# A new order list for a retention and SwiGLU kernel: same operations, other sequence, other engines, other PSUM banks

## The chip, the cores and the metric

The kernel runs on one core of a Trainium2 chip. That core has a matrix engine (TensorE, PE in the profile), three engines that work on tiles (VectorE, or DVE; ScalarE, or ACT; GpSimd, or POOL), a queue engine that only starts transfers (SyncE, or SP), and 16 DMA engines that carry them out. The metric is the device time of one execution in microseconds (us). Less is better.

## The reference

q, k and v have the shape (4 batches, 8 heads, 768 positions, 64 channels). A retention layer runs over the positions, and a SwiGLU block with an RMS norm runs over its output, which is seen as 3072 rows of 512 channels (8 heads x 64):

```python
for t in range(S):                                     # gamma_h = 1 - 2**(-5-h)
    state = gamma * state + einsum('bhd,bhe->bhde', k[:, :, t], v[:, :, t])
    y[:, :, t] = scale * einsum('bhd,bhde->bhe', q[:, :, t], state)
x = y.transpose(0, 2, 1, 3).reshape(3072, 512)
xn = x / sqrt(mean(x * x, -1) + 1e-6) * rms_g
g = xn @ w_gate                                        # 512 x 1536
out = (g * sigmoid(g) * (xn @ w_val)) @ w_out          # 1536 x 512
```

## The kernel before, in words

The positions are cut into six groups c = 0 to 5 of 128 positions. A group has one block of 128 rows per batch b, so one group is 512 rows. Inside a block the recurrence is written as a masked product of scores, and a state per batch carries the past from group to group. The feed-forward block then runs over the 512 rows of the group: twelve slices of 128 hidden channels, each with four matmuls of 128x512 for the gate and four for the value, and then twelve matmuls of 128x512 per batch for the output.

The whole program is one string, ORDER (line 17). It has 867 words, one operation each, and a loop at the end of the function emits them in turn. A word reads `name.c.b/banks@engine>gate`. The numbers behind the name are the group, the batch and further arguments. The digits behind "/" are the PSUM banks that the operation writes. "@D", "@A", "@P" and "@S" stand for DVE, ACT, POOL and SP. ">name" lets a transfer wait for another operation. No planner stands behind it: each engine carries out its own words strictly in the order of the string, and an engine that waits for one word holds back all of its later words. An operation that writes a bank waits for the last reader of that bank, and a tile of a ring in SBUF is reused after its last reader.

The words that this text uses, with the line of the instruction that the profile shows:

- L (Lq, Lk, Lv) loads a block of q, k or v (L312, L314). On SP it arrives in f32 in a ring (four buffers each for q and k, six for v); on POOL the transfer casts to bf16 on its way. wg, wv and wo load slices of the weights, on POOL (L325, L332).
- Cq, Ck and V cast the f32 blocks to bf16, q and v with their decay (L341, L145, L360; V on ACT is eight small activations, L358).
- Tq and Tk transpose on PE (L368 for blocks loaded in another layout, L373), and Eq and Ek evacuate the result. tq and tk are DMA transposes on SP (L389), for the groups from c = 2 on.
- mk0 and mk1 compute the first group's decay masks on ACT (L268) from a row mask that the word iota makes on POOL; mc multiplies the second group's mask (L281); causal makes the 0/1 mask on POOL (L253).
- A computes scores (L405, two banks per batch), M0 and M1 multiply them by the mask on DVE (L427), Y and Z compute the block's output (L442, L446).
- S, R and N are the norm: the squares' sum on ACT (L459), the root on POOL (L469, L471), and the scaled rows on DVE (L483). X and XE transpose those rows into xnT, on PE with an evacuation (L496, L145) in the groups 0 and 1 and as a DMA transpose on SP (L502) from c = 2 on.
- J and D prepare decayed k rows (L518); K, U and B bring the state up to date: matmuls (L529), an f32 sum or copy (L538, L145), a bf16 copy on POOL (L545).
- g and v are the gate and value matmuls (L553), s the Silu on ACT (L563), h the product on DVE (L571), d and e the output matmuls (L578; e, L600, in three cuts for the last block), o the evacuation of the output (L145, on DVE or ACT), st its store (L591). H and tab warm up PE and ACT's table.

`g.0.3.4.0.3/0` is thus the gate product of group 0, hidden slice 3 alone, batches 0 to 2, into bank 0. Group 0's feed-forward work is cut into such pieces, so that it can start before all of its batches are there.

Of the kernel before, what the change touches and what calls it, by code (L numbers as in the profile page):

```python
# [17 lines left out]
Lk.0.2@S H.4/4 yd causal Lv.0.2@S>causal yt rms.1@S ident Ck.0.2@A Lq.0.0@P H.8/1 Lq.0.1@P Lq.0.2@P Tk.0.2/7  # L18
H.2/5 Lk.0.0@P Tq.0.1/0 vd Tq.0.0/4 Ek.0.2@D Lk.0.1@P Tq.0.2/1 Lk.0.3@P G/7 V.0.2@D Eq.0.1@D Tk.0.0/0 Tk.0.1/6
Eq.0.2@D Eq.0.0@D iota Lq.0.3@P A.0.2/31 Lv.0.1@P mk0 Lv.0.0@P Lv.0.3@P Ek.0.0@D mk1 GE@A wg.0.2 M1.0.2 wv.0.2  # L20
H.2/4 M0.0.2 Ek.0.1@A A.0.0/5270 D.0.2@P M1.0.1 Tk.0.3/6 Y.0.2/1 Tq.0.3/0 M0.0.1 H.2/4 tab Lk.1.1@P M1.0.0
M0.0.0 S.0.2 Ek.0.3@A J.0.0/4 J.0.1/7 R.0.2 Y.0.1/2 Eq.0.3@A S.0.1 H.1/6 H.3/0 H.1/5 D.0.0@D Y.0.0/3 N.0.2
J.0.3/5 D.0.1@D wv.2.4 R.0.1 X.0.2/6 N.0.1 S.0.0 wg.2.4 A.0.3/41 R.0.0 X.0.1/0 XE.0.2@A wg.4.6 D.0.3@D M0.0.3
XE.0.1@A g.0.0.2.2.3/2 K.0.2.2/5 K.0.0.2/6 M1.0.3 U.0.2.2@A s.0.0.2.2.3 N.0.0 v.0.0.2.2.3/7 g.0.0.2.1.2/0
h.0.0.2.2.3 Y.0.3/5 Lq.1.0@P wv.4.6 X.0.0/3 U.0.0.2@A S.0.3 wg.6.9 Tk.1.1/4 v.0.0.2.1.2/2 XE.0.0@D s.0.0.2.1.2
h.0.0.2.1.2 g.0.0.2.0.1/6 R.0.3 wv.6.9 Ek.1.1@A v.0.3.4.0.3/3 v.0.2.3.0.3/4 N.0.3 g.0.3.4.0.3/0 Lk.1.2@P
s.0.0.2.0.1 X.0.3/6 v.0.0.2.0.1/5 XE.0.3@A Lk.1.0@P B.0.0 wg.9.12 s.0.3.4.0.3 Lq.1.1@P g.0.5.6.0.3/1
g.0.2.3.0.3/7 h.0.3.4.0.3 s.0.2.3.0.3 Lq.1.2@P h.0.2.3.0.3 g.0.4.5.0.3/0 wv.9.12 h.0.0.2.0.1 s.0.4.5.0.3
v.0.0.4.3.4/2 g.0.0.4.3.4/7 v.0.4.5.0.3/3 mc.1@P s.0.5.6.0.3 s.0.0.4.3.4 h.0.0.4.3.4 wo.0.4 v.0.5.6.0.3/4
# [36 lines left out]
d.2.3.0.12/1 d.2.2.0.12/2 U.3.0.2@D g.3.0.1.0.4/4 v.3.0.1.0.4/7 Lq.4.0@S U.3.2.2@D st.0.2@S g.3.3.4.0.4/0
Ck.4.2@P s.3.3.4.0.4 st.0.1@S Lk.4.3@S Lv.5.0@S g.3.5.6.0.4/3 st.1.1@S B.3.1 v.3.3.4.0.4/0 d.2.1.10.12 tk.4.2
g.3.4.5.0.4/5 Cq.4.3@P Cq.4.1@D s.3.0.1.0.4 Lq.5.3@S o.2.3@A h.3.0.1.0.4 h.3.3.4.0.4 s.3.5.6.0.4 o.2.1@D
g.3.1.2.0.4/3 v.3.1.2.0.4/1 s.3.1.2.0.4 Ck.5.0@D o.2.2@D B.3.2 tq.4.2 V.4.3@P g.3.6.7.0.4/4 Lq.5.2@S V.4.2@P
Cq.4.0@P v.3.6.7.0.4/3 s.3.6.7.0.4 tq.4.0 h.3.1.2.0.4 v.3.5.6.0.4/0 g.3.2.3.0.4/2 h.3.5.6.0.4 Lk.5.1@S  # L70
h.3.6.7.0.4 tk.4.0 s.3.4.5.0.4 V.5.2@P tq.4.1 s.3.2.3.0.4 v.3.2.3.0.4/4 g.3.9.10.0.4/1 Ck.4.3@D v.3.4.5.0.4/0
Ck.5.1@D B.3.0 s.3.9.10.0.4 Lk.5.2@S g.3.10.11.0.4/1 Lk.5.3@S st.2.3@S h.3.4.5.0.4 Cq.5.3@P Lv.4.1@S A.4.0/0352
s.3.10.11.0.4 v.3.10.11.0.4/6 B.3.3 h.3.2.3.0.4 M0.4.0 M1.4.0 M0.4.1 M1.4.1 g.3.8.9.0.4/1 tq.4.3 v.3.9.10.0.4/7
Y.4.0/4 st.1.2@S tk.4.3 s.3.8.9.0.4 S.4.0 v.3.8.9.0.4/5 Cq.5.2@D st.2.1@S h.3.10.11.0.4 h.3.9.10.0.4
d.2.0.0.10/1 Lq.5.1@S R.4.0 N.4.0 Ck.5.2@A V.4.1@A A.4.2/6732 h.3.8.9.0.4 Lq.5.0@S M0.4.2 M1.4.2 Y.4.1/4
g.3.7.8.0.4/5 d.2.0.10.12 g.3.11.12.0.4/6 Cq.5.1@P Ck.5.3@D M1.4.3 K.4.2.2/7 o.2.0@A s.3.7.8.0.4 tq.5.2 M0.4.3
s.3.11.12.0.4 K.4.0.2/1 U.4.2.2@D Z.4.2/50 tq.5.3 v.3.7.8.0.4/2 tk.5.2 Y.4.3.2 Y.4.2.2 S.4.1 h.3.7.8.0.4
# [562 lines left out]
```

## Time and profile before

| | us |
|---|---|
| median of 3 runs | 232.16 (231.90, 232.18 and 232.16) |
| span of the profiled execution | 230.7 |
| what lies around that span, against the median | 1.46 |
| PE busy | 223.7 (97%) |
| DVE, ACT, POOL busy | 128.7, 87.8, 92.8 |
| granted PE clock | 1.00 throughout |

The profile gives the profiled execution's span, from its first to its last instruction; the times of the runs hold what lies around it too, so the two are compared through the difference in the table. The page gives busy times of each engine, the chain of work that ended last (followed back from the last instruction), groups of equal instructions with their mean duration and the idle time ahead of them, and DMA issues with the median time to landing. In a row of the timeline, the first number is the start, the second the duration, and the brackets hold the engine's idle time before it and what ended that. In a row of a table of stretches, the columns are the stretch, its length, and the busy time of PE, PE's weight loads, DVE, ACT and POOL with their numbers of instructions, then the PE clock, the DMA share and GB/s.

### The profile page before, as it was taken

The page shows a single profiled execution, that of the slowest core. Times are in us where ns is not written, and L with a number is a line of the kernel's source. Part 1 is how long each engine was busy: PE and PEld are TensorE (multiplying, and loading weights), DVE is VectorE, ACT ScalarE, POOL GpSimd, SP SyncE. Part 2 cuts the span into 40 slices and gives each one's busy share as a digit, 9 for nine tenths or more (in the row PEclk, how much of TensorE's full clock was granted, in tenths as well). Part 3 has the DMA queues.
Part 4 walks back from the last instruction along what each step waited for, and adds up shares of the span by engine and source line. Part 5 has one row for each costly group of instructions (what it writes and reads, how often), then busy time and mean ns, then how long its engine had stood idle before and what let it go on. Part 6 is the DMA issues. An engine that isn't in the chain of part 4 may idle for free.

```text
span 230.7 us, 4733 instructions
## 1 busy us (share of the span) xinstructions
PE 223.7 (97%) x1822; PEld 119.3 (52%) x1849; DVE 128.7 (56%) x239; ACT 87.8 (38%) x197; POOL 92.8 (40%) x163
## 2 busy tenths in 40 slices
PE   8989999999999999999999999999999999999994
PEld 2567755556564554445544445544554444444552
DVE  5797296937574876476670648856664325432200
ACT  6776524216424450344420435661354124222021
POOL 8979999124866235424349401339040000000000
PEclk9999999999999999999999999999999999999999
DMA  7999999999978946999999989774216200001142
GB/s 132 158 175 122 187 174 192 201 185 239 180 164 186 203 104 172 245 162 248 231 141 263 216 194 227 155 117 99 65 23 190 108 0 0 0 12 38 45 180 93
DMA packets 105353, 33.60 MB, mean 146 GB/s; under 512 B 94450, under 2 KB 102386, under 8 KB 105331
## 3 DMA queue, kind: packets, MB, share of 16 engines
q1 hardware_dynamic: 81858, 25.70, 51.0%
q0 software_dynamic: 23472, 7.60, 30.3%
q8 instruction: 14, 0.23, 0.4%
q14 instruction: 9, 0.07, 0.1%
HBM read 28.31 MB, written 6.29 MB: 150 GB/s over the span
## 4 chain that ended last, share of the span: by engine, by line
PE 93%; DMA 3%; issue 1%; DVE 1%; ACT 0%; POOL 0%; DVEq 0%
PE v_ps L553 26%; PE g_ps L553 26%; PE o_ps L578 26%; DMA wg_b<-in_moe_w_gate_dram 3%; PE hot_ps L239 3%; PE a_ps L405 3%; PE y_ps L442 2%; PE y_ps L446 2%; PE o_ps L600 1%; PE kv_ps L529 1%; PE t_ps L368 1%; PE t_ps L373 1%; DVE am L427 1%; PE xt_ps L496 1%; PE g_row_ps L295 0%
## 5 line engine op out<-in xcount | busy, mean ns | idle before, releaser
L571 DVE TENSOR_TENSOR hT<-sg,v_ps 128x512 bf16<-128x512 bf16 (+2 forms) x76 | 48.0, 655 | 54.4 <-PE v_ps L553 39.8
L563 ACT ACTIVATE sg<-g_ps 128x512 bf16<-128x512 f32 (+2 forms) x76 | 42.4, 575 | 88.8 <-PE g_ps L553 79.1
L553 PE MATMUL g_ps<-xnT,wg_b 128*128 128x512 bf16 (+2 forms) x334 | 70.2, 343 | 0.8 <-DMA wg_b<-in_moe_w_gate_dram 0.4
L553 PE MATMUL v_ps<-xnT,wv_b 128*128 128x512 bf16 (+2 forms) x338 | 70.4, 344 | 0.5 <-issue 0.2
L578 PE MATMUL o_ps<-wo_b,hT 128*128 128x512 bf16 x265 | 62.3, 379 | 0.6 <-issue 0.2
L553 PEld LDWEIGHTS <-wg_b 128*128 128x128 bf16 x344 | 30.6, 98 | 30.3 <-DMA wg_b<-in_moe_w_gate_dram 0.8
L553 PEld LDWEIGHTS <-wv_b 128*128 128x128 bf16 x344 | 30.5, 98 | 29.1 <-DVE hT L571 0.2
L578 PEld LDWEIGHTS <-hT 128*128 128x128 bf16 x276 | 26.3, 98 | 29.7 <-DVE hT L571 0.2
L469 POOL TENSOR_SCALAR ms<-ssq 128x1 f32<-128x1 f32 x24 | 4.5, 189 | 48.8 <-ACT xsq L459 48.0
L427 DVE TENSOR_TENSOR am<-a_ps,causal 128x512 bf16<-128x512 f32 x32 | 20.2, 682 | 3.3 <-PE a_ps L405 3.2
L483 DVE SCALAR_TENSOR_TENSOR xn<-y_ps,rstd,g_bc 128x512 bf16<-128x512 f32 x22 | 16.4, 748 | 9.8 <-POOL rstd L471 8.0
L545 POOL CAST st_b<-st_f 64x256 bf16<-64x256 f32 x40 | 18.7, 467 | 6.7 <-DVE st_f L538 5.4
L459 ACT ACTIVATE xsq<-y_ps 128x512 f32<-128x512 f32 x22 | 13.1, 598 | 15.6 <-PE y_ps L446 14.2
L341 POOL TENSOR_TENSOR qb<-qf,ydec 128x512 bf16<-128x512 f32 x13 | 13.7, 1055 | 10.5 <-DMA qf<-in_q_dram 10.2
L145 ACT COPY o_sb<-o_ps 128x512 f32<-128x512 f32 (+1 forms) x15 | 8.4, 567 | 23.5 <-PE o_ps L578 23.1
L471 POOL TENSOR_TENSOR rstd<-ms,mhalf 128x1 f32<-128x1 f32 x24 | 13.2, 552 | 2.0
L145 DVE COPY o_sb<-o_ps 128x512 f32<-128x512 f32 (+2 forms) x11 | 6.7, 620 | 13.0 <-PE o_ps L578 7.3
L360 POOL TENSOR_TENSOR vp<-vf,vdec 128x512 bf16<-128x512 f32 x9 | 9.3, 1040 | 5.4 <-DMA vf<-in_v_dram 5.3
L427 DVE TENSOR_TENSOR am<-a_ps,mask 128x512 bf16<-128x512 f32 x16 | 9.9, 681 | 1.6 <-PE a_ps L405 1.4
L239 PE MATMUL hot_ps<-one 128*128 128x512 bf16 x23 | 8.4, 516 | 1.1 <-DVE one L152 1.1
L442 PEld LDWEIGHTS <-am 128*128 128x128 bf16 x176 | 7.7, 98 | 3.5
L442 PE MATMUL y_ps<-vp,am 128*128 128x64 bf16 x176 | 8.8, 193 | 0.0
(98 smaller groups left out, 161.0 us busy)
## 6 DMA issues: line engine op xcount, KB each, us to landing
out_dram<-o_sb SPq DMA_DIRECT2D x23, 256.0 KB, 2.4
kf<-in_k_dram SPq DMA_DIRECT2D x17, 256.0 KB, 3.9
vf<-in_v_dram SPq DMA_DIRECT2D x17, 256.0 KB, 4.4
qf<-in_q_dram SPq DMA_DIRECT2D x16, 256.0 KB, 4.0
wo_b<-in_moe_w_out_dram POOLq DMA_DIRECT2D x3, 512.0 KB, 10.7
qb<-in_q_dram POOLq DMA_DIRECT2D x8, 128.0 KB, 5.8
kb<-in_k_dram POOLq DMA_DIRECT2D x7, 128.0 KB, 7.1
vp<-in_v_dram POOLq DMA_DIRECT2D x7, 128.0 KB, 7.4
```

Source lines behind the costliest of these rows:

```text
L145: (e.copy if e is ACT else e.tensor_copy)(out, in_)
L239: nc.tensor.matmul(p, one, one[:, None, :].to_broadcast([128, 4, 128]), start=True, stop=True)
L341: e.tensor_tensor(out=u["qb"], in0=u["qf"], in1=ydec[:, c, :, None].to_broadcast([128, H, D]), op=ALU.mult)
L427: DVE.tensor_tensor(out=u["am"][:, i], in0=u["a"][i], in1=m, op=ALU.mult)
L442: nc.tensor.matmul(y[:, h, :], u["am"][:, h % 2, h // 2, :], u["vp"][:, h, :], start=h == 0, stop=c == 0 and h == H - 1, skip_group_check= ...
L471: POOL.tensor_tensor(out=u["rstd"], in0=ms, in1=mhalf, op=ALU.pow)
L483: DVE.scalar_tensor_tensor(out=u["xn"], in0=flat(u["y"]), scalar=u["rstd"], in1=g_bc, op0=ALU.mult, op1=ALU.mult)
L545: POOL.tensor_copy(st_b[b][r, :, i * 64:i * 64 + 64], st_f[b // 2][r, b % 2])
L553: nc.tensor.matmul(p[:, (n - n0) * m:(n - n0 + 1) * m], W[w][0][:, s, n * 128:(n + 1) * 128], xnT[c][:, s, b0 * C:b1 * C], start=s == 0, s ...
L563: ACT.activation(sg[:, :cols], done["wg", c, n0, b0][:, :cols], AF.Silu)
L571: DVE.tensor_tensor(out=hT[c][:, n0:n1, b0 * C:b1 * C], in0=sg, in1=p, op=ALU.mult)
L578: nc.tensor.matmul(o_ps[c, b], hT[c][:, n, b * C:(b + 1) * C], wo_b[:, n, :], start=n == 0, stop=n == NFF - 1)
```

## The change

ORDER is written anew. The same 867 operations stand in it, with the same arguments. Nothing is added or removed, and shapes and transfers are the same. Up to the word `h.0.8.9.0.4`, some 170 words in, the sequence of the words is the old one. From there on it is a new sequence. Four things differ:

1. The gate of `Lv.0.2@S>causal` is gone.
2. The banks are dealt anew, from the first word on.
3. Engines change. In the first stretch: Ck.0.2 from ACT to DVE, Ek.0.2 from DVE to ACT, V.0.2 from DVE to POOL, U.0.0.2 from ACT to DVE, mc.1 from POOL to DVE, D.1.0 from DVE to POOL. Behind it: ten output evacuations o from ACT to DVE and nine from DVE to ACT (two of these are narrow cuts); XE.1.0 to DVE and XE.1.1 to ACT; Ek.1.2 and Ek.1.0 to ACT; Ck.2.1, 5.0, 5.1 and 5.3 from DVE to ACT, Ck.5.2 from ACT to DVE, Ck.2.2 from POOL to ACT, Ck.3.3, 4.0 and 4.1 from ACT to POOL; five Cq from POOL to DVE and one back; V.2.3 and 5.3 from POOL to ACT, V.3.0 and 3.2 from DVE to ACT, V.5.1 from ACT to DVE, V.2.2, 3.3 and 5.2 from POOL to DVE, V.2.0 from DVE to POOL; D.1.3 from DVE to POOL.
4. From the middle of group 0 on, words stand elsewhere: loads and transposes on SP, casts, mask products and states between the feed-forward words.

The functions are edited only to return their instruction, except that D falls back to the f32 tile of k where there is no other; no instruction comes from that. Cut to the places of which the text speaks:

```diff
-Lk.0.2@S H.4/4 yd causal Lv.0.2@S>causal yt rms.1@S ident Ck.0.2@A Lq.0.0@P H.8/1 Lq.0.1@P Lq.0.2@P Tk.0.2/7
-H.2/5 Lk.0.0@P Tq.0.1/0 vd Tq.0.0/4 Ek.0.2@D Lk.0.1@P Tq.0.2/1 Lk.0.3@P G/7 V.0.2@D Eq.0.1@D Tk.0.0/0 Tk.0.1/6
+Lk.0.2@S H.4/0 yd causal Lv.0.2@S yt rms.1@S ident Ck.0.2@D Lq.0.0@P H.8/1 Lq.0.1@P Lq.0.2@P Tk.0.2/0 H.2/1 Lk.0.0@P
+Tq.0.1/2 vd Tq.0.0/1 Ek.0.2@A Lk.0.1@P Tq.0.2/0 Lk.0.3@P G/3 V.0.2@P Eq.0.1@D Tk.0.0/2 Tk.0.1/4 Eq.0.2@D Eq.0.0@D iota
...
-H.2/4 M0.0.2 Ek.0.1@A A.0.0/5270 D.0.2@P M1.0.1 Tk.0.3/6 Y.0.2/1 Tq.0.3/0 M0.0.1 H.2/4 tab Lk.1.1@P M1.0.0
+A.0.0/4256 D.0.2@P M1.0.1 Tk.0.3/0 Y.0.2/1 Tq.0.3/3 M0.0.1 H.2/6 tab Lk.1.1@P M1.0.0 M0.0.0 S.0.2 Ek.0.3@A J.0.0/5
...
-h.0.0.2.2.3 Y.0.3/5 Lq.1.0@P wv.4.6 X.0.0/3 U.0.0.2@A S.0.3 wg.6.9 Tk.1.1/4 v.0.0.2.1.2/2 XE.0.0@D s.0.0.2.1.2
-h.0.0.2.1.2 g.0.0.2.0.1/6 R.0.3 wv.6.9 Ek.1.1@A v.0.3.4.0.3/3 v.0.2.3.0.3/4 N.0.3 g.0.3.4.0.3/0 Lk.1.2@P
+M1.0.3 U.0.2.2@A s.0.0.2.2.3 N.0.0 v.0.0.2.2.3/5 g.0.0.2.1.2/0 h.0.0.2.2.3 Y.0.3/3 Lq.1.0@P wv.4.6 X.0.0/5 U.0.0.2@D
+S.0.3 wg.6.9 Tk.1.1/2 v.0.0.2.1.2/4 XE.0.0@D s.0.0.2.1.2 h.0.0.2.1.2 g.0.0.2.0.1/5 R.0.3 wv.6.9 Ek.1.1@A v.0.3.4.0.3/0
+v.0.2.3.0.3/2 N.0.3 g.0.3.4.0.3/3 Lk.1.2@P s.0.0.2.0.1 X.0.3/5 v.0.0.2.0.1/4 XE.0.3@A Lk.1.0@P B.0.0 wg.9.12
...
-Ck.5.1@D B.3.0 s.3.9.10.0.4 Lk.5.2@S g.3.10.11.0.4/1 Lk.5.3@S st.2.3@S h.3.4.5.0.4 Cq.5.3@P Lv.4.1@S A.4.0/0352
-g.3.7.8.0.4/5 d.2.0.10.12 g.3.11.12.0.4/6 Cq.5.1@P Ck.5.3@D M1.4.3 K.4.2.2/7 o.2.0@A s.3.7.8.0.4 tq.5.2 M0.4.3
+A.4.0/6347 Lv.5.2@S v.3.3.4.0.4/1 Cq.5.3@D o.2.0@A v.3.9.10.0.4/5 M0.4.0 g.3.10.11.0.4/6 Cq.4.3@P Lk.5.3@S M0.4.1
+h.3.3.4.0.4 v.3.4.5.0.4/1 Ck.5.3@A s.3.4.5.0.4 B.3.3 Lk.5.2@S Lq.5.1@S Lv.4.2@S M1.4.1 V.4.3@P s.3.6.7.0.4
...
-st.4.0@S d.5.1.0.10/0 o.4.3@A st.4.3@S o.5.0@D st.5.0@S d.5.1.10.12 e.5.3.1/6 o.5.1@A st.4.2@S o.5.3.1@D
-d.5.2.0.12/0 st.5.3.2@S st.5.1@S st.5.3.1@S e.5.3.0/1 o.5.2@A st.5.2@S o.5.3.0@A st.5.3.0@S
+o.5.0@A st.4.1@S d.5.2.0.12/2 st.5.1@S o.5.3.2@A o.5.2@A st.5.3.1@S e.5.3.0/6 o.5.3.0@A st.5.0@S st.5.3.2@S st.4.2@S
+st.5.2@S st.5.3.0@S
```

Between the new list's XE.3.3 and Lk.5.3, SP's own words are st.1.2, Lq.4.2, Lv.4.3, tk.4.2, tk.4.0, tq.4.0, st.1.3, Lk.5.0, tk.4.3, tq.4.2, Lq.4.3 and Lv.5.2. On DVE, the words from the product h.2.10.11 to N.3.2 are h.2.10.11, U.3.0.2, Ck.4.3, h.2.11.12 and N.3.2.

More of the change, by code (lines that the diff above doesn't have):

```diff
@@ L144, in copy @@
     def copy(e, out, in_):
-        (e.copy if e is ACT else e.tensor_copy)(out, in_)
+        return (e.copy if e is ACT else e.tensor_copy)(out, in_)
     def flat(x):
@@ L242, in iota @@
     def iota(e, bk):
-        POOL.affine_select(out=row_m, in_=row_f, compare_op=ALU.is_ge, fill=1.0e6, base=0,
+        return POOL.affine_select(out=row_m, in_=row_f, compare_op=ALU.is_ge, fill=1.0e6, base=0,
                            pattern=[[1, C]], channel_multiplier=-1)
@@ L257, in vd @@
     def vd(e, bk):
-        ACT.activation(vdec, darg, AF.Exp, scale=-1.0, bias=zero)
+        return ACT.activation(vdec, darg, AF.Exp, scale=-1.0, bias=zero)
     @op
     def yd(e, bk):
-        ACT.activation(ydec, darg, AF.Exp, scale=1.0, bias=lnscale)
+        return ACT.activation(ydec, darg, AF.Exp, scale=1.0, bias=lnscale)
     def mask(i):
@@ L280, in mc @@
         dec = vdec[:, 1].rearrange("p (hp i) -> p hp i", i=2)[:, :, i:i + 1]
-        e.tensor_tensor(out=mask1[:, i], in0=causal[:, None, :].to_broadcast([128, NHP, C]),
+        return e.tensor_tensor(out=mask1[:, i], in0=causal[:, None, :].to_broadcast([128, NHP, C]),
                         in1=dec.to_broadcast([128, NHP, C]), op=ALU.mult)
@@ L285, in tab @@
     def tab(e, bk):
-        ACT.activation(warm, zero, AF.Silu)
+        return ACT.activation(warm, zero, AF.Silu)
     @op
@@ L298, in GE @@
     def GE(e, bk):
-        copy(e, g_bc, done["G"])
+        return copy(e, g_bc, done["G"])
     def load(n, e, c, b, near=0):
@@ L308, in load @@
         else:
-            x = t[c, b][n + "f"] = ring([128, H, D], F32, n + "f", {"q": 4, "k": 4, "v": 6}[n])
-        if n != "v" and c == 0 and e is POOL and not near:
+            x = t[c, b][n + "f"] = ring([128, H, D], F32, n + "f", RING[n])
+        if n != "v" and c == 0 and (near == 8 if e is SP else not near):
             t[c, b][n + "8"] = True
@@ L338, in Cq @@
         if c == 0:
-            copy(e, u["qb"], u["qf"])
+            return copy(e, u["qb"], u["qf"])
         else:
@@ L346, in Ck @@
         u["kb"] = ring([128, H, D], BF16, "kb", 10)
-        copy(e, u["kb"], u["kf"])
+        return copy(e, u["kb"], u["kf"])
     @op
@@ L383, in E @@
             return
-        copy(e, u[n + "T"], u[n + "P"])
+        return copy(e, u[n + "T"], u[n + "P"])
     def tr(n, c, b):
@@ L388, in tr @@
         u[n + "T"] = ring([128, NHP, 128], BF16, n + "T", 6)
-        SP.dma_start_transpose(out=u[n + "T"], in_=flat(u[n + "b"]))
+        return SP.dma_start_transpose(out=u[n + "T"], in_=flat(u[n + "b"]))
     for n in "qk":
@@ L426, in M @@
         m = (mask0, mask1)[c][:, i] if c <= 1 else causal[:, None, :].to_broadcast([128, NHP, 128])
-        DVE.tensor_tensor(out=u["am"][:, i], in0=u["a"][i], in1=m, op=ALU.mult)
+        return DVE.tensor_tensor(out=u["am"][:, i], in0=u["a"][i], in1=m, op=ALU.mult)
     F["M0"] = lambda e, bk, c, b: M(0, c, b)
@@ L458, in S_ @@
         u["ssq"] = ring([128, 1], F32, "ssq", 4)
-        ACT.activation(xsq, flat(u["y"]), AF.Square, accum_out=u["ssq"])
+        return ACT.activation(xsq, flat(u["y"]), AF.Square, accum_out=u["ssq"])
     @op
@@ L470, in R @@
         u["rstd"] = ring([128, 1], F32, "rstd", 4)
-        POOL.tensor_tensor(out=u["rstd"], in0=ms, in1=mhalf, op=ALU.pow)
+        return POOL.tensor_tensor(out=u["rstd"], in0=ms, in1=mhalf, op=ALU.pow)
     @op
@@ L482, in N @@
             return
-        DVE.scalar_tensor_tensor(out=u["xn"], in0=flat(u["y"]), scalar=u["rstd"], in1=g_bc,
+        return DVE.scalar_tensor_tensor(out=u["xn"], in0=flat(u["y"]), scalar=u["rstd"], in1=g_bc,
                                  op0=ALU.mult, op1=ALU.mult)
@@ L501, in XE @@
         if e is SP:
-            SP.dma_start_transpose(out=x, in_=t[c, b]["xn"])
+            return SP.dma_start_transpose(out=x, in_=t[c, b]["xn"])
         else:
-            copy(e, x, t[c, b]["xP"])
+            return copy(e, x, t[c, b]["xP"])
     @op
@@ L535, in U @@
         if c == 0:
-            copy(e, x, t[c, b]["kv"])
+            return copy(e, x, t[c, b]["kv"])
         else:
-            DVE.tensor_tensor(out=x, in0=x, in1=t[c, b]["kv"], op=ALU.add)
+            return DVE.tensor_tensor(out=x, in0=x, in1=t[c, b]["kv"], op=ALU.add)
     @op
@@ L562, in s_ @@
         sg = done["s", c, n0, b0] = ring([128, GT], BF16, "sg", 3)
-        ACT.activation(sg[:, :cols], done["wg", c, n0, b0][:, :cols], AF.Silu)
+        return ACT.activation(sg[:, :cols], done["wg", c, n0, b0][:, :cols], AF.Silu)
     @op
@@ L570, in h_ @@
         sg, p = (done[w, c, n0, b0][:, :(n1 - n0) * m].rearrange("p (n t) -> p n t", t=m) for w in ("s", "wv"))
-        DVE.tensor_tensor(out=hT[c][:, n0:n1, b0 * C:b1 * C], in0=sg, in1=p, op=ALU.mult)
+        return DVE.tensor_tensor(out=hT[c][:, n0:n1, b0 * C:b1 * C], in0=sg, in1=p, op=ALU.mult)
     @op
@@ L585, in o @@
             done["o", c, b] = ring([128, DM], F32, "o_sb", 6)
[L586 removed]
+        return copy(e, done["o", c, b] if i is None else done["o", c, b][:, CUT[i]:CUT[i + 1]], p)
     @op
```

153 lines of the change are left out of this document (75 added, 78 removed).

## The prediction

> **What bounds the kernel now.** I read the page first, then the span in three stretches, then what TensorE (PE) waits for, then the chain of work that ended last.
>
> ```profile
> span 230.7 us, 4733 instructions
> ...
> PE 223.7 (97%) x1822; PEld 119.3 (52%) x1849; DVE 128.7 (56%) x239; ACT 87.8 (38%) x197; POOL 92.8 (40%) x163
> ...
> PE 93%; DMA 3%; issue 1%; DVE 1%; ACT 0%; POOL 0%; DVEq 0%
> ```
> ```profile
> 0.00:22.83 22.83, 20.61 (x314) 12.78 (x314) 17.10 (x56) 16.27 (x38) 20.21 (x40) 1.00 1.25 147
> 22.83:227.55 204.72, 203.08 (x1509) 106.50 (x1536) 111.59 (x183) 71.22 (x158) 72.61 (x124) 1.00 0.78 146
> 227.55:230.70 3.15, 0.00 (x0) 0.00 (x0) 0.00 (x0) 0.32 (x1) 0.00 (x0) 1.00 0.32 114
> ```
> ```profile
> PE hot_ps L239 <- DVE one L152: 1.1, 1, 1.1
> PE g_ps L553 <- DMA wg_b<-in_moe_w_gate_dram: 0.4, 1, 0.4
> PE xt_ps L496 <- DVE xn L483: 0.4, 1, 0.4
> PE t_ps L368 <- DVE am L427: 0.2, 1, 0.2
> ```
> ```profile
> 16.16 6.63 DMA wg_b<-in_moe_w_gate_dram
> ...
> 186.04 2.59 PE g_ps L553 x12
> ```
>
> PE is 97% busy and is 93% of the chain. The middle stretch is 204.72 us with 203.08 busy at clock 1.00, and the waits that the profile names there add up to tenths. A 128x512 matmul streams in 2.59 / 12 = 0.216 us. The list keeps every operation and every shape, so this stretch cannot get shorter. It can only get longer, by a new PE wait. What can be won lies before 22.83, where the chain runs through one weight transfer, issued at 16.16 and landed 6.63 later (22.79), and in the last 3.15 us. The sum is made against this execution: span 230.7, and 232.16 - 230.7 = 1.46 us around it for the median of the runs shown; I add a change of the span to 232.16.
>
> **The front (0 to 22.83).**
>
> ```profile
> 0.79 0.45 SPq L314 DMA_DIRECT2D kf<-in_k_dram  x1
> ...
> 1.27 0.37 POOL L253 TENSOR_SCALAR_AFFINE_SELECT causal<-causal 128x128 bf16<-128x128 bf16 x1
> ...
> 1.67 0.39 SPq L314 DMA_DIRECT2D vf<-in_v_dram  x1
> ...
> 6.26 2.74 POOL L314 DMA_DIRECT2D vp<-in_v_dram  x3
> ...
> 7.22 0.42 DVE L145 CAST vp<-vf 128x512 bf16<-128x512 f32 x1
> ```
> ```profile
> 13.30 0.18 POOL L469 TENSOR_SCALAR ms<-ssq 128x1 f32<-128x1 f32 x1 [0.89 <-ACT xsq L459]
> ```
> ```profile
> 20.00 0.42 DVE L145 COPY xnT<-xt_ps 128x512 bf16<-128x512 bf16 x1 [0.24 <-PE xt_ps L496]
> ...
> 21.98 0.75 DVE L483 SCALAR_TENSOR_TENSOR xn<-y_ps,rstd,g_bc 128x512 bf16<-128x512 f32 x1 [0.73 <-POOL rstd L471]
> ```
>
> The gate of Lv.0.2 goes. It was issued at 1.67, behind causal's end at 1.27 + 0.37 = 1.64; SP was free at 0.79 + 0.45 = 1.24. So it goes out 0.4 earlier. What follows it from memory can move by 0 to 0.4; I take 0.2. Tq.0.3 leaves the bank that a mask product (am) still read, so PE's 0.2 wait (t_ps <- DVE am) goes too. Both lie ahead of the norms that release R.0.1, behind which POOL issues the weight transfer at 16.16. Together 0.2 to 0.45, taken at 0.3.
>
> Against it: V.0.2 moves from DVE (0.42) to POOL, an estimated 0.6 (the ACT cast of the same size takes 0.61), ahead of the row mask and nine issues; POOL's 0.89 of idle time before 13.30 takes that up. Without that idle time it would be +0.6 on the weight transfer, but PE idles 0.4 in front of it. U.0.0.2 moves to DVE ahead of the evacuation at 20.00. As a 128x512 f32 copy it is 0.69 (row below) against 0.24 of idle time, so XE.0.0 is 0.45 later less the 0.3 just won. That eats into the 0.4 that PE waits for the weights, and costs nothing on top. Ek.0.2 on ACT puts the masks behind it by an ACT copy (0.59, row below). I cost it at nothing, because the first mask product waits for the first scores, and these for three DVE casts; with that cover gone it would be +0.6.
>
> There is one new limit. g.0.3.4 now takes the bank that Y.0.3 held until N.0.3 has read it. In the old trace N.0.3 ends at 21.98 + 0.75 = 22.73, against 22.79 for the weights. So the weights could come much earlier and PE would still wait for N.0.3, which moves only with the norms. **Front: -0.3, between -0.45 and +0.2.** The upper end is U.0.0.2 uncovered with nothing won ahead of it.
>
> The trace speaks on one more thing here, the DVE casts beside POOL's issuing. V.0.2's cast (7.22, 0.42) lay inside POOL's three issues (6.26 to 9.00, 0.91 each), and a later issue without such a cast took 0.89 (row: 18.65, below), so nothing was held up. The Trainium skill, "SBUF — State Buffer", section "Who interferes with whom", says the contrary may happen: a DVE cast in a two-port mode locks the port pair that GpSimd shares, and GpSimd's descriptor writing waits it out. Ck.0.2 now does that cast on DVE among POOL's first issues, so by that rule the software stream would start up to one cast (0.45) later and the front would come out near +0.15, not -0.3; the row decides for me.
>
> ```profile
> 18.65 0.89 POOL L314 DMA_DIRECT2D qb<-in_q_dram  x1
> ```
>
> **The middle (204.7 us).** What changes is who evacuates and who casts.
>
> ```profile
> L563 ACT ACTIVATE sg<-g_ps 128x512 bf16<-128x512 f32 x64 | 37.2, 597 | 84.1 <-PE g_ps L553 76.4 <-DVE hT L571 5.0 <-PE v_ps L553 1.4
> ...
> L145 ACT COPY o_sb<-o_ps 128x512 f32<-128x512 f32 x14 | 8.1, 585 | 23.1 <-PE o_ps L578 23.1
> L145 ACT CAST kb<-kf 128x512 bf16<-128x512 f32 x8 | 4.9, 613 | 1.4 <-DMA kf<-in_k_dram 1.4
> ```
> ```profile
> L145 DVE COPY o_sb<-o_ps 128x512 f32<-128x512 f32 x9 | 6.1, 685 | 7.5 <-PE o_ps L578 7.3
> ```
> ```profile
> 28.75 1.69 DVE L571 TENSOR_TENSOR hT<-sg,v_ps 128x512 bf16<-128x512 bf16 x3 [1.66 <-ACT sg L563]
> 30.35 1.72 DVE L281 TENSOR_TENSOR mask<-causal,vdec 128x512 f32<-128x512 bf16 x1
> ```
> ```profile
> kf<-in_k_dram SPq DMA_DIRECT2D x17, 256.0 KB, 3.9
> vf<-in_v_dram SPq DMA_DIRECT2D x17, 256.0 KB, 4.4
> ```
> ```profile
> 119.48 1.22 SPq L502 DMA_TRANSPOSE xnT<-xn  x1
> 120.75 0.57 SPq L314 DMA_DIRECT2D qf<-in_q_dram  x1
> ```
>
> Seventeen full evacuations and two narrow ones of the output trade places (ten from ACT to DVE, the others back): 10 x 0.685 onto DVE and 7 x 0.585 onto ACT. With the casts, the decayed v's and mc.1 I count DVE about +3, ACT about +6 and POOL about -5 us. That leaves DVE near 132, ACT near 94 and POOL near 88, all far from 223.7. No engine becomes the bound; only places can. mc.1 as a DVE operation is 1.72, as mc.0 is at 30.35, and falls into the idle 1.66 before 28.75: at most 0.06 late, on a product that PE does not wait for at once. D.1.0 goes to POOL in its stead.
>
> The banks are dealt anew, so each PE group waits for another reader. For each I set the group's place on PE (0.216 per full matmul) against the end of its bank's last reader (0.60 ACT, 0.69 DVE, in the order of their lists). Nearly all have more than half a us; the tightest (A.1.3, d.1.3, K.2.0, A.1.0, Z.4.2) come out at 0.2 to 0.25 late. The old list gives up to 0.3 late by the same count, and its trace shows no wait there, so this is the error of the count. I take +0.1 for them (0 to +0.5) and 0 to +0.15 for the smaller groups (scores, states) standing next to other neighbours, taken with it.
>
> One place depends on a transfer. Ck.5.3, the cast of the last k, was a DVE cast some way behind its load; now it stands on ACT ahead of s.3.4.5, s.3.6.7 and s.3.10.11, and its load Lk.5.3 is late on SP. Behind g.3.2.3 stand 368 full matmuls (79.4), the three cut groups of the end (about 3.0) and fourteen small groups (about 0.4 each, 5.6), so it starts near 227.5 - 88.0 = 139.5, and g.3.9.10 another four matmuls later, at 140.3. The latter takes the bank that s.3.10.11 reads. Ahead of that end stand the cast (0.61) and three Silus (1.79), so the cast must start by 137.9. On SP, XE.3.3 ends about 123.1: N.3.2 is near 119.9 on DVE behind two products, a state update and a cast, 0.75 of its own, then two transposes of 1.22. Then come five transposes at 1.22 and seven loads or stores at 0.5 to 0.57, 9.9 to 10.6 with their gaps: Lk.5.3 is issued at 133.1 to 133.7 and lands, at the median 3.9, at 137.0 to 137.6. That is 0.3 to 0.9 ahead of need; at the 4.4 of the v loads the later end is 0.2 behind it. I take 0, with +1.5 as the upper end (a load of 5.5).
>
> **The tail (3.15 us).** o.5.3.0, the one ACT instruction (0.32) of the last stretch, and its store end the span. The new list puts the stores of o.5.0, o.5.3.2 and o.4.2 right ahead of the last two, so one 256 KB store more may be under way beside the last. Bounds: 0 and one issue of 0.57; I take +0.1.
>
> **Sum.** -0.3 + 0.1 + 0 + 0.1 = -0.1: 232.06, said as 232.1. The likeliest case's own range: -0.45 to +0.45, 231.7 to 232.6.
>
> **Rivals.** (1) Slower: Ck.5.3 waits for Lk.5.3 and holds ACT, so g.3.2.3 and g.3.9.10 wait for their banks. It decides from a landing at about 137.9 on, and each tenth later is a tenth on the time. For it: the margin is under a us, and the loads' medians run from 3.9 to 4.4. Against it: PE's earlier front moves need and load together. Price +0.5 to +1.5, taken at 0.9: 232.0 + 0.9 = 232.9. (2) Slower: the count's late banks are real. Two of the five at 0.25, and the front's gain used up by N.0.3: +0.5 to +0.8, 232.8. Against it: the same count is too strict for the old list. (3) Faster: the front gives its full 0.45 and all other terms are 0, or the new neighbours cost less: 231.6. For it: PE's named waits in the front (0.4, 0.4, 0.2) are that large; against it: N.0.3's bank. (4) The ungated load changes nothing, or POOL is held up, since other terms hide it: 232.2 to 232.5.
>
> **Numbers.** Runs of this kernel lie within 0.28 us of each other, so 0.2% (0.46 us) is about what a measurement can tell from no change: 231.70 to 232.62. Chances: likeliest 0.36 and rival 4 0.06 (same, 0.42); rival 3 0.20 (faster); rival 1 0.24 and rival 2 0.14 (slower, 0.38). The range goes from 231.4 (rival 3 with a little of the tail) to 233.6 (rival 1 at its upper end), leaving out about 0.05 below and 0.1 above.
>
> **What would show it.** Right: Lv.0.2 issued near 1.25, g.0.3.4 near 22.5 with a wait of a few tenths for weights or N.0.3, no PE wait over 0.2 behind it, Ck.5.3 starting before 137.9. Wrong: ACT idle for DMA kf near 137 with PE waiting for ACT sg behind it (rival 1); PE waits for DVE or ACT in many places (rival 2); a front that ends at 22.8 or later (rival 4). The prediction would also fail if SP's chain of loads, each in order behind the other, drifts by more than a us anywhere, since casts in the new list stand closer behind their loads.

## The result, and the profile after

The changed kernel takes 234.50 us (median of 6 runs, 234.12 to 235.57) against 232.31 for the kernel before (6 runs, 231.90 to 233.75). The ratio is 1.0092, with a 95% interval of 1.0068 to 1.0115: slower by 0.9%, about 2.1 us. I had forecast 232.1, too close to 232.16 to be told from no change, with a range of 231.4 to 233.6.

The profiled execution took 235.57 us, with a span of 233.7. It is the slowest of the six, so its waits may be longer than those of a usual execution. So 1.87 us lie around the span here, where I had worked with 1.46 for the kernel before. That figure subtracted one execution's span from the median of others, and is not exact to better than some tenths. In the experiments it is 1.7 to 2.0. The line numbers shift by a few from kernel to kernel: L553, the gate and value matmuls of the kernel before, is L551 here and L547 to L550 below.

The page's busy times and the same stretches as before, cut at the place that matters (columns: stretch, length, busy PE, weight loads, DVE, ACT, POOL with their instructions, clock, DMA share, GB/s):

```profile
PE 225.8 (97%) x1849; PEld 119.0 (51%) x1849; DVE 129.2 (55%) x239; ACT 92.0 (39%) x222; POOL 86.3 (37%) x159
...
PE 85%; DMA 7%; POOL 2%; SPq 2%; DVE 1%; issue 1%; ACT 0%; ACTq 0%; DVEq 0%
```
```profile
0.00:22.79 22.79, 20.78 (x313) 12.82 (x314) 17.09 (x56) 15.60 (x37) 21.34 (x41) 1.00 1.27 150
22.79:139.50 116.71, 116.08 (x948) 62.35 (x949) 70.14 (x116) 44.81 (x107) 48.37 (x83) 1.00 1.05 187
139.50:142.70 3.20, 1.07 (x6) 0.43 (x5) 0.98 (x2) 1.88 (x4) 3.00 (x6) 1.00 0.93 212
142.70:230.60 87.90, 87.89 (x586) 43.41 (x584) 41.02 (x66) 29.42 (x74) 13.55 (x32) 1.00 0.31 83
230.60:233.70 3.10, 0.00 (x0) 0.00 (x0) 0.00 (x0) 0.32 (x1) 0.00 (x0) 1.00 0.33 116
```

The front (22.79 against 22.83) and the tail (3.10 against 3.15) are what they were. The clock is 1.00 throughout, and no engine has become the bound. PE's share of the chain fell from 93% to 85% and that of transfers rose from 3% to 7%. In the 3.2 us behind 139.5, PE is busy for 1.07. What PE waits for (us in total, times, longest):

```profile
PE g_ps L551 <- ACT sg L562: 2.1, 1, 2.1
PE hot_ps L236 <- DVE one L149: 1.1, 1, 1.1
PE y_ps L440 <- DVE am L425: 0.6, 1, 0.6
PE xt_ps L494 <- DVE xn L481: 0.5, 1, 0.5
PE g_ps L551 <- DMA wg_b<-in_moe_w_gate_dram: 0.4, 1, 0.4
```

Two waits are new: 2.1 us for a Silu on ACT and 0.6 us for a mask product on DVE. The chain that ended last shows where the larger one comes from (start, duration, what), and the timeline of ACT and PE shows the two ends of it:

```profile
132.92 1.21 SPq L387
134.13 0.05 issue
134.18 0.57 SPq L311
134.75 0.05 issue
134.81 0.91 SPq L311
135.72 0.04 issue
135.76 4.96 DMA kf<-in_k_dram
```
```profile
140.82 0.62 ACT L142 CAST kb<-kf 128x512 bf16<-128x512 f32 x1 [5.32 <-DMA kf<-in_k_dram]
...
141.34 1.56 ACT L562 ACTIVATE sg<-g_ps 128x512 bf16<-128x512 f32 x3
...
141.99 2.00 PE L551 MATMUL g_ps<-xnT,wg_b 128*128 128x512 bf16 x8 [2.13 <-ACT sg L562]
```

This is Lk.5.3, issued at 135.76 and landed 4.96 later. Ck.5.3 has held ACT idle for 5.32 us, the three Silus s.3.4.5, s.3.6.7 and s.3.10.11 follow at once behind it, and g.3.2.3 starts at 141.99. It is the prediction's first rival, at its place. The smaller wait is of the same kind, on DVE:

```profile
109.69 0.69 DVE L358 TENSOR_TENSOR vp<-vf,vdec 128x512 bf16<-128x512 f32 x1 [0.87 <-DMA vf<-in_v_dram]
110.30 1.88 DVE L425 TENSOR_TENSOR am<-a_ps,causal 128x512 bf16<-128x512 f32 x3
```

V.3.3 waits 0.87 us for Lv.3.3, and the mask products listed behind it come late; the first one's bank is the one that Y.3.1 takes. In the old list V.3.3 stood on POOL.

### The profile page after: what moved, and what is told of

Read it like the earlier page. It is cut to its first block, busy times and chain, and to the rows that moved or that the text cites. A ratio compares the mean times of both kernels' runs of the same rounds, so it can differ in the third digit from the quotient of the medians.

```text
span 233.7 us, 4766 instructions
## 1 busy us (share of the span) xinstructions
PE 225.8 (97%) x1849; PEld 119.0 (51%) x1849; DVE 129.2 (55%) x239; ACT 92.0 (39%) x222; POOL 86.3 (37%) x159
## 4 chain that ended last, share of the span: by engine, by line
PE 85%; DMA 7%; POOL 2%; SPq 2%; DVE 1%; issue 1%; ACT 0%; ACTq 0%; DVEq 0%
PE g_ps L551 25%; PE o_ps L577 25%; PE v_ps L551 22%; DMA wg_b<-in_moe_w_gate_dram 3%; PE hot_ps L236 2%; DMA kf<-in_k_dram 2%; PE y_ps L440 2%; PE a_ps L403 2%; PE y_ps L444 2%; DMA vf<-in_v_dram 1%; PE o_ps L599 1%; PE kv_ps L527 1%; SPq L387 1%; PE t_ps L371 1%; DVE qT L142 1%
## 5 line engine op out<-in xcount | busy, mean ns | idle before, releaser
L551 PE MATMUL g_ps<-xnT,wg_b 128*128 128x512 bf16 (+2 forms) x344 | 71.0, 345 | 2.5 <-ACT sg L562 2.1
L551 PE MATMUL v_ps<-xnT,wv_b 128*128 128x512 bf16 (+2 forms) x344 | 70.3, 345 | 0.0
L577 PE MATMUL o_ps<-wo_b,hT 128*128 128x512 bf16 x276 | 63.2, 379 | 0.0
L551 PEld LDWEIGHTS <-wg_b 128*128 128x128 bf16 x344 | 30.5, 98 | 32.1 <-issue 2.6
L551 PEld LDWEIGHTS <-wv_b 128*128 128x128 bf16 x344 | 30.5, 98 | 29.4
L339 POOL TENSOR_TENSOR qb<-qf,ydec 128x512 bf16<-128x512 f32 x9 | 9.9, 1098 | 26.6 <-DMA qf<-in_q_dram 22.8
L543 POOL CAST st_b<-st_f 64x256 bf16<-64x256 f32 x40 | 16.8, 420 | 5.8 <-DVE st_f L536 4.3
L142 ACT COPY o_sb<-o_ps 128x512 f32<-128x512 f32 (+2 forms) x14 | 7.2, 526 | 20.3 <-PE o_ps L577 19.5
L142 DVE COPY o_sb<-o_ps 128x512 f32<-128x512 f32 x12 | 8.0, 685 | 5.9 <-PE o_ps L577 5.9
L142 ACT CAST kb<-kf 128x512 bf16<-128x512 f32 x8 | 4.8, 614 | 15.9 <-DMA kf<-in_k_dram 15.9
L356 ACT ACTIVATE vp<-vf,vdec 128x64 bf16<-128x64 f32 x40 | 10.1, 339 | 0.0
```

The costliest lines, as they stand in the source:

```text
L142: return (e.copy if e is ACT else e.tensor_copy)(out, in_)
L543: POOL.tensor_copy(st_b[b][r, :, i * 64:i * 64 + 64], st_f[b // 2][r, b % 2])
L551: r = nc.tensor.matmul(p[:, (n - n0) * m:(n - n0 + 1) * m], W[w][0][:, s, n * 128:(n + 1) * 128], xnT[c][:, s, b0 * C:b1 * C], start=s == ...
L577: nc.tensor.matmul(o_ps[c, b], hT[c][:, n, b * C:(b + 1) * C], wo_b[:, n, :], start=n == 0, stop=n == NFF - 1)
```

## The experiments

My theory after the result: the loss is made by casts that stand in an engine's list ahead of work that PE needs, and that wait for a load late in SP's chain. The rivals: the many new bank and engine places cost, each a little; or the new front does.

**One word moved: the cast behind the Silus.**

```diff
-Ck.5.3@A
 s.3.4.5.0.4
...
 s.3.9.10.0.4
+Ck.5.3@A
```

> The changed list with one word moved: Ck.5.3, the cast of k's last block, goes on ACT from ahead of s.3.4.5 to behind s.3.9.10; nothing else differs. Theory (the cast's wait for its load holds three Silus, and PE waits for their banks): the PE wait of 2.1 us at g.3.2.3 is gone, Ck.5.3 starts near 144 without a wait, and the time falls by about 2 us from the changed kernel's profiled run, 1.2 to 2.4 against its median of 234.5, to 232.2 to 233.2. Rival (the last load of the SP chain is late for everything, or PE is held up by the many new places): the wait reappears a few us later at the next user, and less than 0.5 us is won.

Measured: 233.88 us, ratio to the kernel before 1.0059 (1.0036 to 1.0082). The wait at g.3.2.3 is gone, as the theory had it, but the time falls by 0.6 us (0.3%) only, short of the forecast 1.2 to 2.4, and the two intervals overlap. The profile shows a second wait of PE in its place, 1.1 us at v.3.11.12, and its cause on DVE:

```profile
PE v_ps L550 <- DVE hT L569: 1.1, 1, 1.1
```
```profile
147.43 0.69 DVE L338 TENSOR_TENSOR qb<-qf,ydec 128x512 bf16<-128x512 f32 x1 [2.22 <-issue]
148.04 0.68 DVE L569 TENSOR_TENSOR hT<-sg,v_ps 128x512 bf16<-128x512 bf16 x1
```

That is Cq.5.2. It stands ahead of the product h.3.7.8, and DVE had been idle for 2.22 us when it started at 147.43. The row names no releaser ("issue"), but its load Lq.5.2 landed at 147.35, right ahead of it. In the changed kernel the 2.1 us wait had covered this one: there Cq.5.2 starts at 147.69 with no idle time before it. So the time won was less than the wait removed.

**One letter: V.3.3 on POOL.**

```diff
-V.3.3@D
+V.3.3@P
```

> The changed list with one letter changed: V.3.3 goes from DVE to POOL, so its wait for Lv.3.3 no longer stands ahead of four mask products on DVE. Theory: the PE wait of 0.63 us at Y.3.1 (about 111 us) goes, and the wait at g.3.2.3 stays: 0.4 to 0.7 us faster than the changed kernel, 233.8 to 234.1. Rival (the 0.63 us is taken up by the later, longer wait, since SP's transfers do not get earlier): no change of the time, with the wait at g.3.2.3 longer by the same 0.6.

Measured: 234.17 us, ratio 1.0089 (1.0063 to 1.0114). The wait at Y.3.1 is gone from the profile and that at g.3.2.3 is there:

```profile
PE g_ps L550 <- ACT sg L561: 1.6, 1, 1.6
```

The ratio is that of the changed kernel within its interval, so what the smaller wait costs alone isn't resolved. The rival's time (no change) fits, but its mechanism is not shown: it wanted the wait at g.3.2.3 longer by 0.6, and that is 0.5 shorter than in the changed kernel's profile.

**Both.**

> The changed list with both edits, Ck.5.3 behind s.3.9.10 on ACT and V.3.3 on POOL. Theory (these two waits are the whole loss): 231.9 to 232.5, no slower than the kernel before, with no PE wait over 0.3 us behind 23 us. Rival (the new neighbours and banks cost as well): 232.8 or more.

Measured: 232.64 us, ratio 1.0017 (0.9992 to 1.0043). The time can't be told from that of the kernel before; it lies between the theory's 232.5 and the rival's 232.8. PE's waits behind 23 us are 0.2 and less (the first row's wait, for xn, is at 17.0):

```profile
PE xt_ps L493 <- DVE xn L480: 0.5, 1, 0.5
PE v_ps L550 <- DVE hT L569: 0.2, 1, 0.2
PE v_ps L550 <- issue: 0.2, 1, 0.2
```

Two edits take back 0.75 of the 0.92%. All other new places, banks and engines together cost at most what the interval leaves, 0.4%. The two edits together win more than the sum of what each won alone (0.33% and 0.03%), because the 1.1 us at v.3.11.12 are 0.2 here. Cq.5.2 stands where it stood, but DVE waits 1.31 us for it instead of 2.22. Why its load was less late against PE's work is left open.

**The cause put into the kernel before.**

```diff
-s.3.9.10.0.4 Lk.5.2@S
-g.3.10.11.0.4/1 Lk.5.3@S
+Lk.5.2@S Lk.5.3@S Ck.5.3@A s.3.9.10.0.4
+g.3.10.11.0.4/1
...
-Ck.5.3@D
```

> The kernel before with the suspected cause put in: Ck.5.3 goes from DVE to ACT and stands there ahead of s.3.9.10; Lk.5.2 and Lk.5.3 are written ahead of it, with SP's own sequence unchanged. In the trace of before s.3.9.10 starts at 136.81 and Lk.5.3 lands at 138.62, and g.3.10.11, which takes the bank s.3.9.10 reads, starts at 137.26. Theory: ACT waits until about 138.6, the cast and the Silu end near 139.8, and PE waits about 2.5 us at g.3.10.11: 234.4 to 235.0. Rival (PE's place in the order gives slack that such a wait falls into): under 0.5 us slower than before.

Measured: 234.52 us, ratio 1.0113 (1.0079 to 1.0147). The profile has PE waiting 2.0 us at g.3.10.11 and ACT idle for the load:

```profile
PE g_ps L548 <- ACT sg L558: 2.0, 1, 2.0
```
```profile
137.97 0.62 ACT L140 CAST kb<-kf 128x512 bf16<-128x512 f32 x1 [2.81 <-DMA kf<-in_k_dram]
138.50 0.59 ACT L558 ACTIVATE sg<-g_ps 128x512 bf16<-128x512 f32 x1
```

The loss of 2.1 us is that of the changed kernel, as the theory had it. With removal and insertion agreeing on PE's wait, the cast that stands ahead of the Silus and waits for its load is shown as the cause of the 2 us.

**The load's place on SP.** Two doses: behind Lk.5.0, ahead of two transposes and two loads; and ahead of the two loads only. The cast stays where the change put it.

```diff
 Lk.5.0@S
+Lk.5.3@S
 tk.4.3
...
 tq.4.2
...
-Lk.5.3@S
```

> The changed list with one word moved on SP: Lk.5.3 goes ahead of tk.4.3, tq.4.2, Lq.4.3 and Lv.5.2, to right behind Lk.5.0. Ck.5.3 stays where it is on ACT. Theory (the load's place on SP against the cast's place on ACT is the cause): Lk.5.3 is issued near 131.5 and lands near 135.5, Ck.5.3 starts near 137 with no wait, and the 2.1 us at g.3.2.3 go: 232.2 to 233.6, with the wait of 0.6 to 0.85 at Y.3.1 left. Rival (the cast's place on ACT itself costs, whenever its load lands): PE still waits about 0.5 to 1 us at g.3.2.3 and g.3.9.10.

Measured: 232.96 us, ratio 1.0014 (0.9987 to 1.0040). PE doesn't wait at g.3.2.3, and the time is as the theory had it. What is left is 0.4 us at Y.3.1 and 0.6 us at v.3.11.12.

```diff
 tq.4.2
+Lk.5.3@S
...
 Lq.4.3@S
...
 Lv.5.2@S
...
-Lk.5.3@S
```

> The changed list with Lk.5.3 moved ahead of only two loads on SP, Lq.4.3 and Lv.5.2. In the changed kernel Lq.4.3 was issued at 134.18 and landed at 139.05, Lk.5.3 at 135.76 with its cast's start at 140.82. Theory A (what counts is the place in the pack of loads that share the queue): Lk.5.3 is issued near 134.2 and lands 0.9 per load earlier, near 139.0; the cast starts 1.8 earlier and the PE wait at g.3.2.3 falls from 2.1 to 0.2 to 0.6; 233.0 to 233.8. Theory B (this load is slow for itself, whatever stands ahead of it): the wait stays over 1 us and the time within 0.4 of 234.5.

Measured: 233.30 us, ratio 1.0035 (1.0014 to 1.0057). The timeline of SP's issues and of ACT:

```profile
133.36 0.57 SPq L310 DMA_DIRECT2D kf<-in_k_dram  x1
133.99 0.57 SPq L310 DMA_DIRECT2D qf<-in_q_dram  x1
134.60 0.99 SPq L310 DMA_DIRECT2D vf<-in_v_dram  x1
135.64 0.94 SPq L310 DMA_DIRECT2D kf<-in_k_dram  x1
136.62 2.38 SPq L310 DMA_DIRECT2D qf<-in_q_dram  x1
```
```profile
136.71 0.62 ACT L141 CAST kb<-kf 128x512 bf16<-128x512 f32 x1 [1.63 <-DMA kf<-in_k_dram]
```

As the first of the pack, Lk.5.3 lands 3.3 us after its issue and the cast starts at 136.71, as the prediction's "before 137.9" wanted; PE no longer waits at g.3.2.3. It is better than theory A's own number: the landing is 4.1 us earlier (140.72 to 136.63), 2.4 of it by the issue (135.76 to 133.36) and 1.7 by the time from issue to landing. The qf load that is now second, Lq.4.3, lands 5.1 us after its issue. The issues also grow longer along the pack, from 0.57 for the first two to 2.38 for the fifth. The time is still 0.35% over that of the kernel before, though no wait of PE behind 23 us is over 0.3. And V.3.3, which stands on DVE here, waits only 0.26 us for its load, and PE not at all at Y.3.1: that smaller wait comes and goes with the load's landing (0.6, 0.85 and 0.4 us in the other three profiles with V.3.3 on DVE).

**The front.** The gate alone, in the kernel before:

```diff
-Lv.0.2@S>causal
+Lv.0.2@S
```

> The kernel before with one thing changed: Lv.0.2 is not gated by causal. My prediction's step: Lv.0.2 is issued near 1.3 instead of 1.67, the first scores come 0.2 us earlier, and the time falls by 0 to 0.4 us. Rival (the weights' landing, not the norms, ends the front): no change, 231.9 to 232.6, with the group after g.0.3.4 (for instance g.0.7.8) at the place that the landing of wg.2.4 gives.

Measured: 232.65 us, ratio 1.0002 (0.9977 to 1.0026). There is no change, though the interval of over 0.5 us either way could hide a step of 0.2. The load went out at 1.30, but in the profiled execution the first scores were later, at 10.73, since PE waited for the second transfer of q by POOL's queue, the first that it needs:

```profile
8.04 1.08 PE L362 MATMUL t_ps<-pick,qb 128*64 128x64 bf16 x48 [1.09 <-DMA qb<-in_q_dram]
```

That transfer landed at 7.99 here and between 6.5 and 7.3 in the twelve other profiles, so its landing varies by more than the step is worth.

The old front (all words up to h.0.8.9.0.4 as in the kernel before) ahead of the new list with both repairs:

> The e3_both kernel with the front of the kernel before: the words up to h.0.8.9.0.4 (the same words in the same sequence, with the old gate, engines and banks), behind them the new list with its two repairs. My prediction's step (the new front is 0.3 us the faster): 0.3 slower than e3_both, g.0.7.8 near 33.1 against 32.8. The rival, formed on the run with the old front where the weights came early (g.0.7.8 at 32.30 there, 32.75 to 33.05 with the new front): the old front is the faster by 0.3 to 0.5 where the weights land before 22, so 231.9 to 232.4 and g.0.7.8 near 32.3 to 32.5.

Measured: 232.69 us, ratio 1.0011 (0.9989 to 1.0033), the same as with the new front. So neither forecast came true. Inside, the old front is the faster one: g.0.3.4 starts at 21.98 and g.0.7.8 at 32.27, against 32.87 with the new front. But at A.1.0 they stand at 39.62 and 39.68. PE waits 0.4 us at v.0.6.7, whose bank holds a transpose that DVE evacuates, and the rest goes in smaller places.

Then the bank that I had named a new limit. Banks 3 and 6 are traded in every word from g.0.3.4 on, and Cq.5.2 goes to POOL:

```diff
-g.0.3.4.0.3/3
+g.0.3.4.0.3/6
...
-g.0.5.6.0.3/6
+g.0.5.6.0.3/3
...
-Cq.5.2@D
+Cq.5.2@P
```

> The e3_both kernel with banks 3 and 6 traded from g.0.3.4 on, so that g.0.3.4 no longer takes the bank that N.0.3 reads, and with Cq.5.2 on POOL instead of DVE. Theory (N.0.3's bank holds g.0.3.4 back when the weights land early): g.0.3.4's first matmul comes before N.0.3's end, the front is 0.1 to 0.4 us shorter (g.0.7.8 near 32.4 to 32.6), and no DVE cast waits near 147: 231.9 to 232.5. Rival (VectorE's later evacuations hold the front, not the bank): g.0.7.8 stays at 32.8 and the time at 232.6.

Measured: 232.38 us, ratio 0.9994 (0.9970 to 1.0018). g.0.7.8 comes at 32.48 instead of 32.87, as the theory had it; the time can't be told from that of the kernel with both repairs. The first two rows below are from the kernel with the load ahead of two loads, which has the new front as the change made it, and show the limit. The third is the front with traded banks, from the kernel described last:

```profile
21.73 0.75 DVE L480 SCALAR_TENSOR_TENSOR xn<-y_ps,rstd,g_bc 128x512 bf16<-128x512 f32 x1 [0.61 <-POOL rstd L468]
```
```profile
22.53 0.81 PE L550 MATMUL g_ps<-xnT,wg_b 128*128 128x384 bf16 x4 [0.15 <-DVE xn L480]
```
```profile
22.18 0.81 PE L550 MATMUL g_ps<-xnT,wg_b 128*128 128x384 bf16 x4
```

N.0.3 ends at 22.48 and g.0.3.4 follows at 22.53. With the other bank it starts at 22.18, ahead of N.0.3's end. The profile of the kernel with traded banks and Cq.5.2 on POOL shows yet another cast that waits, Ck.5.2 on DVE, with PE waiting 0.5 us for a Silu at v.3.6.7:

```profile
140.31 0.78 DVE L141 CAST kb<-kf 128x512 bf16<-128x512 f32 x1 [2.47 <-DMA kf<-in_k_dram]
141.01 0.68 DVE L569 TENSOR_TENSOR hT<-sg,v_ps 128x512 bf16<-128x512 bf16 x1
```

**All casts behind the work that PE needs.** Ck.5.2 goes behind h.3.6.7 on DVE, once on the old front (with v.0.6.7 in bank 7) and once on the new front with traded banks.

```diff
-Ck.5.2@D
...
 h.3.6.7.0.4
+Ck.5.2@D
```

> The e6_front_before kernel (front of the kernel before, behind it the new list with its two repairs) with the three waits taken away that the last profiles show: v.0.6.7 goes to bank 7 instead of 2, so that it does not wait for Ek.1.2; Cq.5.2 goes to POOL; Ck.5.2 goes on DVE from ahead of h.3.4.5 to behind h.3.6.7. Theory (the old front is 0.5 us the faster, and each wait of an in-order engine for a load is a loss of its own): no PE wait over 0.3 us behind 23 us, last matmul's end near 226.6 to 226.9, 231.6 to 232.1, faster than the kernel before by 0.2 to 0.3%. Rival (what the front wins is lost again at the next tight bank): 232.3 to 232.7.

> The e8_banks_swapped kernel (the new list with its repairs, banks 3 and 6 traded from g.0.3.4 on, Cq.5.2 on POOL) with Ck.5.2 moved on DVE from ahead of h.3.4.5 to behind h.3.6.7. Theory: the PE wait of 0.54 at v.3.6.7, which came from Ck.5.2 waiting for Lk.5.2 and holding h.3.4.5 and so s.3.9.10, goes: last matmul's end near 226.8, 231.7 to 232.2. Rival: the wait comes back at the next user (h.3.7.8) and nothing is won: 232.3 to 232.6.

Measured on the old front: 232.14 us, ratio 0.9999 (0.9978 to 1.0021). PE's last matmul ends at 227.05, against 227.54 in the kernel before and 226.6 to 226.9 forecast, and the time can't be told from that of the kernel before, where the theory wanted it faster. On the new front: 231.97 us against 232.40, ratio 0.9984 (0.9969 to 0.9998). The last matmul ends at 226.96, and PE's only waits over 0.2 us are the first and the one for xn at 16.7. This version is 2.5 us faster than the changed kernel. Against the kernel before it is 0.16% faster, with an interval that ends just short of no change; as one of eleven comparisons, that small gain is likely rather than shown.

## Why the prediction was wrong

**The bound** was read rightly: the list could only lose by new PE waits, and the edits that remove two of them take back the loss, but for what the interval hides (at most 0.4%).

**The front, -0.3.** In the one profile of the changed kernel its steps came as told and the term still failed. Lv.0.2 was issued at 1.31, the first scores came at 10.04 instead of 10.21, R.0.1 and the weight transfer at 15.85 instead of 16.16, and N.0.3 ended at 22.45. But the weights landed at 22.74 (22.78 before): 0.31 earlier in, 0.04 earlier out. The steps themselves aren't shown to come from the change: three further profiles of the old front, its gate in place, have the first scores at 9.96 to 10.08 and the issue at 15.90 to 16.03, and eight of the new front 9.79 to 10.33 and 15.85 to 15.99. I had taken the landing as the issue plus 6.63. In the other profiles of the new front the same transfer, issued at 15.85 to 15.99, landed between 20.9 and 21.6. So one trace's landing is no fixed latency, and an issue moved by 0.3 tells little. Where it landed early, N.0.3's bank, which I had named, held g.0.3.4; the trade of banks gave 0.4 back at g.0.7.8. A hold-up of POOL by the cast of Ck.0.2, which I had put at up to 0.45 (the cast's row has 0.42) and set aside, did come, at 0.32 (last section), but the front came out at -0.04 and not at the +0.15 that I had worked out for it.

**The place that depends on a transfer, 0.** This is the step that failed. I had the place and the mechanism right, and the deadline (137.9) to some tenths: PE came to g.3.2.3 at 139.86 (141.99 less its wait) instead of 139.5, and the cast with its three Silus took 2.1 instead of 2.4. The landing was wrong: 137.0 to 137.6 forecast, 140.7 measured (issue 135.76, 4.96 to landing). The start of the chain was right: XE.3.3 ended at 123.42, forecast 123.1. Two terms were mis-sized. First, the twelve transfers between it and Lk.5.3 took 12.3 us instead of the forecast 9.9 to 10.6, 2 us more: tk.4.2 alone took 2.40 where I had put 1.22, Lv.5.2 took 0.91, and the gaps between them add up to 0.9. Secondly, the load took 5.0 instead of 3.9. I had used medians over the whole kernel for a stretch in which loads stand in a pack, and the trace of before has both tails (a k block's issue of up to 1.90, a landing of up to 5.0). The changed kernel's view of the k blocks gives minimum, median and maximum, in ns for the issue and in us for the landing:

```profile
L311 SPq DMA_DIRECT2D kf<-in_k_dram x17: 382/575/2582, 0.8 to 136.4; - x17
...
DMA to landing us min/median/max: 3.0/4.1/5.2
```

The bound of +1.5 for this term was worked out from a load of 5.5 us alone, with no error on the chain in front of it; chain and load together were 3.1 to 3.7 us later than forecast, which started the cast 2.9 behind the deadline and cost PE 2.1.

**The DVE count, +0.1.** The five tight bank places that I had named cost no more than 0.15 us (K.2.0, in some of the experiments). The 0.6 us at Y.3.1 was not among them: V.3.3 waits for a transfer, and my count had covered bank readers by their engines' times only. I named casts that stand closer behind their loads among what would make the prediction fail, and gave it no term.

**The tail, +0.1,** was 3.10 against 3.15: nothing. **The engines' totals** came out 2 to 3 us under the count (DVE 129.2 for 132, ACT 92.0 for 94, POOL 86.3 for 88), and none is near PE, which was all that the count was for.

**The chances.** Rival 1 had 0.24 and +0.5 to +1.5. Its margin was written as 0.3 to 0.9 us on a chain of thirteen transfers, each with a spread of tenths and more; so narrow a margin on so long a chain deserved more than 0.24. Nor were the 0.28 us between three runs a measure of the spread: the six runs of the kernel before lie 1.85 apart.

## What to carry to other kernels

In a list that an engine works off in order, an operation that waits for a transfer is safe only behind the work that the bottleneck needs next; put casts last among what is free to wait. Cost a chain of transfers by the slow rows of a pack, not by medians over the kernel, and let the margin grow with the number of transfers in it. When a wait is removed, look for the one that it covered: here four casts waited for their loads (V.3.3, Ck.5.3, Cq.5.2 and Ck.5.2), and the last two held PE up only in kernels where an earlier wait had been removed.

## What the runs showed of the hardware

**An issue on SP takes longer when loads are under way.** Over both kernels' SP queues behind 47.5 us, a load's issue takes 0.60 us on the mean with none or one earlier load not yet landed (41 cases), 0.80 with two (30) and 1.26 with three or more (22). A DMA transpose takes 1.22, 1.34, 1.40 and 1.67 with none, one, two and three or more. For ten of the 93 loads the trace has no landing; it is put 4.1 us behind the issue, the changed kernel's median for k, so single cases may be a class off. What holds the issue was not tried apart.

**A cast on DVE did hold POOL's issuing.** I had set aside the rule on the shared port pair, by the row of V.0.2's cast. In the new front Ck.0.2 is cast on DVE at 4.31. The changed kernel's rows of that cast and of POOL's three issues of k at that time:

```profile
4.31 0.40 DVE L142 CAST kb<-kf 128x512 bf16<-128x512 f32 x1
```
```profile
3.90 1.98 POOL L309 DMA_DIRECT2D kb<-in_k_dram  x3
```

In the kernel before, with that cast on ACT, the same three take 1.65:

```profile
3.89 1.65 POOL L312 DMA_DIRECT2D kb<-in_k_dram  x3
```

The issue under way during the cast takes 0.94 instead of 0.62, in every profile of the new front (eight kernels, 0.94 or 0.95) and in none of the old (five: 0.61 or 0.62). This agrees with the Trainium skill, "SBUF — State Buffer", section "Who interferes with whom": GpSimd's descriptor writing waits for a DVE cast that holds the pair. The delay of 0.3 us was not to be seen in the time here; the first scores came 0.17 earlier all the same.

The other order is on record too. V.0.2's cast beside POOL's issues of v takes 0.42 us in the kernel before, but 0.58 in the kernel with the gate alone taken out and 0.79 in the one with Ck.5.3 put ahead of s.3.9.10, while the issue beside it keeps its 0.97:

```profile
6.68 0.79 DVE L140 CAST vp<-vf 128x512 bf16<-128x512 f32 x1
```

There the cast was the one held, as far as the rows show. So the one row of V.0.2 from which I took that nothing is held up was too little to go by.
